# A third fp32 load on the hardware queue at the start, and a planned order with other rules for PSUM banks, scores and values

## The chip, the core and the metric

The kernel runs on one core of a Trainium2 chip. A core has five engines that run side by side, each with its own instruction stream: TensorE (PE in the profile, its weight loads PEld) multiplies matrices and writes to PSUM, VectorE (DVE) and ScalarE (ACT) work on elements and read PSUM, GpSimd (POOL) and SyncE (SP) here mostly issue DMA transfers. PSUM has 8 banks per partition; a bank holds one 128x512 fp32 result. Engines wait for each other by semaphores.

The metric is the time of one execution on the device in microseconds (us), the median of several runs. Before the change it is 298.91 us, with runs from 298.06 to 298.91.

## What is computed

Sliding-window causal attention over 8 batches, 8 heads, 576 positions and a head size of 64, followed by a feed-forward block with silu on the 4608 tokens:

```python
scores = scale * np.matmul(q, k.transpose(0, 1, 3, 2))
rel = pos[:, None] - pos[None, :]
scores = np.where((rel >= 0) & (rel < 64), scores, -1e9)
attn = softmax(scores)                       # per row
x = np.matmul(attn, v)  ->  tokens x 512     # heads side by side
h = x @ w_in                                 # 512 -> 2048
out = (h * sigmoid(h)) @ w_out               # 2048 -> 512, fp32
```

Inputs are fp32 in DRAM; the kernel multiplies in bf16.

## The kernel before, in words

**Attention.** The window is 64 wide, so a block of 64 queries needs two blocks of keys. A unit is three query blocks of a batch. For batches 1 to 7 a unit takes all eight heads: 48 small matmuls of scores into four banks (`scores`, L331), four exps on ACT (`expo`, L337), four masks on DVE (L340), two times 24 matmuls of values (`values`, L349) into two banks, then reciprocal, product and a transposition on DVE (L356, L359, L363) that leave the result, turned, in the SBUF tile `bridge`. Batch 0 takes one half of the heads at a time and adds its mask as a matmul of a bias (L311) ahead of the scores (L319).

**How q and k of batch 0 arrive.** Two heads of q or k are one tensor of 128 rows; there are four such tensors of q and four of k. Those of heads 0 and 1 are loaded by SP's hardware queue as fp32 rows into `nat` tiles (`load_first`, L232) and cast to bf16 on ACT or DVE (`cast_first`, L235). The other six are loaded by POOL's software queue, which casts on the way (`load_first_cast`, L229). Two tensors at a time are turned by PE (`turn_first`, L282) and copied out of PSUM (`lift`, L289). Later batches come through POOL (`load_rows`, L239) and are turned by DVE (L246). POOL also loads v (L253), w_in (L259) and w_out (L265). It issues a load only once the eighth load before it has landed.

**Feed-forward block.** Tokens are taken in nine tiles of 512. For a tile the first layer makes 16 groups of four matmuls (`first_layer`, L369), each group into one bank; ACT empties the bank with a silu into a tile `g` (`silu`, L375). The second layer then makes four groups of 16 matmuls (`second_layer`, L381); ACT or DVE copies each bank out (L387) and SP stores it (L391). The first two tiles are cut into narrower groups. The first layers of the nine tiles appear in the profile as nine stretches of first-layer matmuls.

**What sets the order.** The kernel holds a small planner, the class `Plan`. Every piece of work is added with a class, an assumed time on each engine that may do it, the pieces it depends on, and for PE work a pool of PSUM banks. `Plan.run` steps through assumed time: whenever an engine is free, it takes the piece of the best rank whose dependencies are seen, whose gate lets it pass, and for which its pool has enough idle banks. The instructions are then issued in that order. On the chip the order is fixed; only semaphores decide when each instruction starts. Assumed times thus act on the order and on the choice of banks, not on the waits themselves.

Banks 0 to 3 are named `at`, 4 to 7 `mp`. Scores of later batches take `at`; values take the pool `pv`, which is banks mp0 and mp1; the feed-forward block takes the pool `mp`, all four of mp0 to mp3, and prefers mp2 and mp3. Of the idle ones it takes the one idle the longest. In the kernel before, once no values are left to plan, every piece may take any of the eight banks. From tile 2 the silus and copies count as seen 0.22 us after their assumed end; before, 0.08 us.

Two gates place scores and values between the matmuls of the feed-forward block. `scores_may_run` lets a unit's scores run when enough second-layer matmuls are left in the tile (`more`: 14, or 3 for the first unit of batch 3 and later). `values_wait` holds scores back while values are ready; `values_may_run` holds values from batch 2 on back until the scores may follow them, or until few second-layer matmuls are left. Between the units PE is filled up with feed-forward matmuls of the tile before.

In the first 17 us PE runs matmuls on a blank tile whenever nothing else is ready (`warm`, L612).

## Time and profile before

| | |
|---|---|
| median of 3 runs | 298.91 us (298.06 to 298.91) |
| profiled execution, its own time | 298.06 us |
| its span in the profile | 296.3 us |
| granted TensorE clock, mean | 0.999 |
| PE busy, 3609 matmuls | 285.1 us |
| ACT busy | 176.2 us |
| DVE busy | 138.6 us |
| POOL busy | 117.8 us |
| first-layer matmuls into mp banks (L369) | 109.8 us |
| second-layer matmuls into mp banks (L381) | 99.4 us |
| POOL's software queue | 18.07 MB, 65.9% of 16 engines' span |
| SP's hardware queue | 10.03 MB, 9.5% |

A line of the timeline gives the start in us from the span's start, the duration, the engine, the line of the kernel, the operation, the tile written and the tiles read, shapes and the number of instructions merged into it; in brackets stands how long the engine was idle before it and who ended that. The end of a matmul is modelled (a 128x512 one shows 0.38 us, while the next starts 0.216 us after it), so a busy PE row can overlap the next. Idle time of less than 0.15 us is not listed. In the chain of waits each row is a start, a duration and what ran; "issue" is time in which nothing that the profile shows was waited for. In the list of waits the numbers are total us, how many, and the longest.

### The profile page before, as it was taken

The numbers are of one execution on the slowest core, as the hardware profiler recorded it, in microseconds if no ns is written. First come the engines' busy times: TensorE is split into PE (matmuls) and PEld (weight loads), VectorE is DVE, ScalarE is ACT, GpSimd is POOL, SyncE is SP. The second block draws the span as 40 slices with busy tenths as digits, with TensorE's granted clock in tenths as the row PEclk, the third lists the DMA queues.
The fourth block names the chain that finished last, engine by engine and source line by source line (L and its number), as shares of the span: only waits on it lengthen the run. The fifth ranks groups of instructions, "written<-read, shape, count | busy, mean of one in ns | idle before, by whom it ended". The sixth has DMA issues, their size and how long they took to land.

```text
span 296.3 us, 8502 instructions
## 1 busy us (share of the span) xinstructions
PE 285.1 (96%) x3609; PEld 150.2 (51%) x3641; DVE 138.6 (47%) x340; ACT 176.2 (59%) x340; POOL 117.8 (40%) x175
## 2 busy tenths in 40 slices
PE   8989999899999999999999999999999999999996
PEld 4566644775444544445444454455445444444444
DVE  3682488987885379367922791075205300000000
ACT  5788655787367746764578438753767176217512
POOL 8977896979898968970500000000000000000000
PEclk9999999999999999999999999999999999999999
DMA  8999999999999999993910110011101100010012
GB/s 168 170 201 172 151 160 171 233 138 136 175 176 131 116 177 156 143 117 85 124 28 3 40 71 35 2 38 73 38 0 38 73 35 3 35 71 35 2 71 72
DMA packets 82982, 28.64 MB, mean 97 GB/s; under 512 B 72448, under 2 KB 78208, under 8 KB 82944
## 3 DMA queue, kind: packets, MB, share of 16 engines
q0 software_dynamic: 77184, 18.07, 65.9%
q1 hardware_dynamic: 5760, 10.03, 9.5%
q8 instruction: 28, 0.46, 0.7%
q14 instruction: 10, 0.08, 0.1%
HBM read 36.70 MB, written 9.44 MB: 156 GB/s over the span
## 4 chain that ended last, share of the span: by engine, by line
PE 81%; DMA 7%; POOL 7%; issue 3%; ACT 1%; POOLq 0%; ACTq 0%
PE mp L369 30%; PE mp L381 29%; PE at L381 8%; PE at L369 6%; PE mp L349 3%; PE at L331 3%; DMA w_in_sb<-in_moe_w_in_dram 3%; DMA w_out_sb<-in_moe_w_out_dram 2%; DMA vv<-in_v_dram 2%; POOL nat L239 2%; POOL vv L253 2%; POOL w_out_sb L265 1%; POOL natb L229 1%; POOL w_in_sb L259 1%; ACT ot L387 0%
## 5 line engine op out<-in xcount | busy, mean ns | idle before, releaser
L369 PE MATMUL mp<-bridge,w_in_sb 128*128 128x512 bf16 (+5 forms) x612 | 109.8, 337 | 2.3 <-ACT g L375 0.8
L381 PE MATMUL mp<-w_out_sb,g 128*128 128x512 bf16 (+2 forms) x450 | 99.4, 370 | 4.3 <-issue 3.3
L369 PEld LDWEIGHTS <-w_in_sb 128*128 128x128 bf16 x696 | 66.6, 98 | 61.0 <-issue 2.4
L375 ACT ACTIVATE g<-mp 128x512 bf16<-128x512 f32 (+5 forms) x153 | 77.2, 514 | 24.8 <-PE mp L369 23.6
L381 PEld LDWEIGHTS <-g 128*128 128x128 bf16 x608 | 56.3, 98 | 62.5 <-issue 1.3
L337 ACT ACTIVATE e<-at 128x384 bf16<-128x384 f32 x90 | 38.0, 495 | 24.8 <-PE at L331 24.3
L239 POOL DMA_DIRECT2D nat<-in_k_dram x56 | 34.6, 631 | 13.2 <-DMA vv<-in_v_dram 6.9
L340 DVE TENSOR_TENSOR e<-e,mask 128x384 bf16<-128x384 bf16 x84 | 25.3, 346 | 24.6 <-ACT e L337 24.4
L253 POOL DMA_DIRECT2D vv<-in_v_dram x32 | 31.9, 1016 | 9.7 <-PE mp L349 8.4
L239 POOL DMA_DIRECT2D nat<-in_q_dram x56 | 35.1, 649 | 1.6 <-DMA w_in_sb<-in_moe_w_in_dram 1.3
L387 ACT COPY ot<-mp 128x512 f32<-128x512 f32 (+2 forms) x28 | 15.8, 568 | 33.3 <-issue 16.2
L356 DVE RECIPROCAL rc<-mp 128x6 f32<-128x6 f32 x43 | 7.8, 189 | 39.3 <-PE mp L349 38.7
L381 PE MATMUL at<-w_out_sb,g 128*128 128x512 bf16 (+1 forms) x126 | 25.6, 359 | 0.1
L363 DVE STREAM_TRANSPOSE bridge<-ox 128x384 bf16<-128x384 bf16 x48 | 24.8, 553 | 0.0
L246 DVE STREAM_TRANSPOSE kt<-nat 128x576 bf16<-128x576 bf16 x28 | 20.7, 783 | 6.3 <-DMA nat<-in_k_dram 6.3
L246 DVE STREAM_TRANSPOSE qt<-nat 128x576 bf16<-128x576 bf16 x28 | 20.9, 787 | 3.5 <-DMA nat<-in_q_dram 3.4
L359 DVE TENSOR_TENSOR ox<-mp,rc 128x384 bf16<-128x384 f32 x43 | 21.5, 539 | 0.1
L369 PE MATMUL at<-bridge,w_in_sb 128*128 128x512 bf16 x84 | 19.3, 379 | 0.0
L387 ACT COPY ot<-at 128x512 f32<-128x512 f32 (+1 forms) x8 | 4.4, 546 | 20.7 <-PE at L381 20.7
L349 PEld LDWEIGHTS <-e 128*32 128x32 bf16 x1152 | 11.1, 95 | 9.3 <-issue 5.5
L375 ACT ACTIVATE g<-at 128x512 bf16<-128x512 f32 x21 | 12.3, 597 | 4.8 <-PE at L369 4.8
L349 PE MATMUL mp<-vv,e 128*32 128x65 bf16 x1032 | 12.9, 194 | 0.3 <-ACT e L337 0.2
(57 smaller groups left out, 122.7 us busy)
## 6 DMA issues: line engine op xcount, KB each, us to landing
out_dram<-ot SPq DMA_DIRECT2D x35, 256.0 KB, 2.0
vv<-in_v_dram POOLq DMA_DIRECT2D x32, 144.0 KB, 5.6
nat<-in_q_dram POOLq DMA_DIRECT2D x56, 72.0 KB, 4.5
nat<-in_k_dram POOLq DMA_DIRECT2D x56, 72.0 KB, 4.1
w_out_sb<-in_moe_w_out_dram POOLq DMA_DIRECT2D x8, 256.0 KB, 6.2
w_in_sb<-in_moe_w_in_dram POOLq DMA_DIRECT2D x6, 256.0 KB, 7.3
w_in_sb<-in_moe_w_in_dram POOLq DMA_DIRECT2D x4, 128.0 KB, 5.9
natb<-in_q_dram POOLq DMA_DIRECT2D x3, 144.0 KB, 4.8
```

Source lines behind the costliest of these rows:

```text
L239: nc.gpsimd.dma_start(out=nats[i][32 * h:32 * h + 32].rearrange("p (m x) -> p m x", m=NB), in_=(q, k)[kk][b, 4 * a + h].rearrange("(m p r) ...
L246: nc.vector.transpose(out=to[:, (2 * a + part) * S:(2 * a + part + 1) * S].rearrange("x (m t r) -> x m r t", t=32, r=2), in_=nats[i].rearr ...
L253: queue[e].dma_start(out=vv[b % NV][:, 2 * g0 + 1:2 * g1 + 1:2, 0:D], in_=v[b].rearrange("h s d -> (h s) d").rearrange("(g p) d -> p g d", ...
L337: nc.scalar.activation(out=es[n % NE], in_=at_six(bank), func=ACTF.Exp, scale=scale)
L340: nc.vector.tensor_mul(es[n % NE], es[n % NE], mask0 if g == 0 else mask)
L349: nc.tensor.matmul(at_pv(bank)[32 * h:32 * h + 32, x, t], lhsT=e_of(b, a, n, h)[:, x, 32 * t:32 * t + 32], rhs=vv[b % NV][:, (4 * a + h) * ...
L359: nc.vector.tensor_mul(oxs[n % NOX], at_pv(bank)[:, :, :, 0:D], rcs[n % NRC].unsqueeze(3).to_broadcast([128, 3, 2, D]))
L363: nc.vector.transpose(out=bridge[:, n0:n0 + 3, 2 * a:2 * a + 2].rearrange("x t s (u i) -> x t s u i", u=2), in_=oxs[n % NOX].rearrange("p ...
L369: nc.tensor.matmul(banks[bank["bank"][0]][:, 0:hi - lo], lhsT=w_in_sb[:, c, ft * 128:(ft + 1) * 128], rhs=bridge[:, (j * TT + lo) // 64:(j ...
L375: nc.scalar.activation(out=gts[gt][:, lo:hi], in_=banks[bank["bank"][0]][:, 0:hi - lo], func=ACTF.Silu)
L381: nc.tensor.matmul(banks[bank["bank"][0]][:, 0:hi - lo], lhsT=gts[gt][:, m * 128:(m + 1) * 128], rhs=w_out_sb[:, f, lo:hi], start=(f == 0) ...
L387: copies[e](out=ots[ot][:, lo:hi], in_=banks[bank["bank"][0]][:, 0:hi - lo])
```

## The change

Six things change:

1. `load_first` takes the pair of heads as an argument, and the first three entries of `FIRST_LOADS` (q of heads 0 and 1, k of heads 0 and 1, q of heads 2 and 3) go through SP's queue and are cast on ACT or DVE. The class "early" covers the four that follow.
2. In the planner, an SP load of the start is never slowed by POOL's transfers, counts as seen 0.5 us after its transfer instead of 1.2, and the assumed transfer is 0.69 us for all three.
3. Work takes banks from its own pool to the end; the switch to all eight banks goes.
4. Silus and copies count as seen 0.08 us after their assumed end in all tiles.
5. Scores run while more than 14 second-layer matmuls are left, for every unit; `values_wait` goes.
6. Values have no gate.

The order is planned anew with this, so instructions move on all engines.

```diff
-                            idle = [i for i in self.pools[op["pool"] if head["pv"] < len(self.queues["pv"]) else "all"] if i not in kept and self.done(self.banks[i])]
+                            idle = [i for i in self.pools[op["pool"]] if i not in kept and self.done(self.banks[i])]
...
-                        busy = pipe[True] > begin
+                        busy = pipe[True] > begin and c != "ld0"
...
-                        op["seen"] = pipe[False] + {"ld0": 1.2, "st": 1.2}.get(c, 3.0)
+                        op["seen"] = pipe[False] + {"ld0": 0.5, "st": 1.2}.get(c, 3.0)
...
-    def load_first(i, kk):
-        nc.sync.dma_start(out=nats[i][:, 0:2 * S].bitcast(FP32), in_=two(0, kk))
+    def load_first(i, u, kk):
+        nc.sync.dma_start(out=nats[i][:, 0:2 * S].bitcast(FP32), in_=two(u, kk))
...
-    def scores_may_run(whole, more):
+    def scores_may_run(whole):
...
-        return rest > (more if whole else 6)
+        return rest > (14 if whole else 6)
...
-    def next_of(ops):
...
-    def values_wait(b):
-        pv = next_of(p.queues["pv"])
-        return b > 2 and pv is not None and p.done(pv["deps"])
-
-    def values_may_run():
-        s, op = next_of(p.queues["s"]), next_of(op for op, _, _ in moe[scores_may_run.i:])
-        if s is None or op is None or not p.done(op["deps"]):
-            return True
-        kind, rest = next((kind, rest) for o, kind, rest in moe[scores_may_run.i:] if o is op)
-        return kind == 2 and rest < 5 or p.done(s["deps"]) and scores_may_run(True, s["more"])
...
-            if u == 0:
+            if (what, u) in FIRST_LOADS[0:3]:
...
-                ld = p.add("ld0", {"SP": 0.45}, lambda _, i=i, kk=kk: load_first(i, kk), dma=-0.15 if kk == 0 else 0.7)
+                ld = p.add("ld0", {"SP": 0.45}, lambda _, i=i, u=u, kk=kk: load_first(i, u, kk), dma=0.69)
...
-                ca = p.add("early" if (what, u) in FIRST_LOADS[2:6] else "dma0", {"POOL": 0.6}, lambda _, w=w, u=u, kk=kk: load_first_cast(w, u, kk), dma=0.74)
+                ca = p.add("early" if (what, u) in FIRST_LOADS[3:7] else "dma0", {"POOL": 0.6}, lambda _, w=w, u=u, kk=kk: load_first_cast(w, u, kk), dma=0.74)
...
-        more = 3 if b > 2 and g == 0 else 14
...
-                  lat=0.1, gate=lambda: scores_may_run(whole, more) and not values_wait(b), pool="at" if b else "all", b=b, nb=2 * na)
-        s["more"] = more
+                  lat=0.1, gate=lambda: scores_may_run(whole), pool="at" if b else "all", b=b, nb=2 * na)
...
-                   gate=values_may_run if b > 1 else None,
...
-                            silu(bank, g, lo, hi), [op] + free_gt.get(g, []), lat=0.22 if j > 1 else 0.08, table="silu"))
+                            silu(bank, g, lo, hi), [op] + free_gt.get(g, []), table="silu"))
...
-                           [op, free_ot.get(ot)], lat=0.22 if j > 1 else 0.08)
+                           [op, free_ot.get(ot)])
```

## The prediction, on record before the result

> **What bounds the kernel now.** I read the page first: shares by engine, then the costliest groups.
>
> ```profile
> PE 285.1 (96%) x3609; PEld 150.2 (51%) x3641; DVE 138.6 (47%) x340; ACT 176.2 (59%) x340; POOL 117.8 (40%) x175
> ...
> L375 ACT ACTIVATE g<-mp 128x512 bf16<-128x512 f32 (+5 forms) x153 | 77.2, 514 | 24.8 <-PE mp L369 23.6
> ```
>
> TensorE (PE) fills the span, and the silu evictions of L375 wait for it. So a change is worth what it adds to or takes from PE's waits. Next, PE's waits from 83 us to the end:
>
> ```profile
> PE mp L381 <- issue: 2.4, 15, 0.2
> PE mp L369 <- issue: 0.2, 1, 0.2
> ```
>
> No line names another engine. In these 213 us there is nothing left to gain, and every new wait is paid in full. Before 83 us there are such waits; the timeline of the start shows them:
>
> ```profile
> 9.86 0.47 PE L282 MATMUL at<-ident,natb 128*64 128x128 bf16 x9 [0.28 <-DMA natb<-in_k_dram]
> ...
> 17.59 1.73 PE L369 MATMUL mp<-bridge,w_in_sb 128*128 128x192 bf16 x16 [0.41 <-DVE bridge L363]
> 19.97 1.25 PE L369 MATMUL mp<-bridge,w_in_sb 128*128 128x192 bf16 x13 [0.65 <-DMA w_in_sb<-in_moe_w_in_dram]
> ...
> 42.14 1.02 PE L381 MATMUL mp<-w_out_sb,g 128*128 128x512 bf16 x4 [0.28 <-DMA w_out_sb<-in_moe_w_out_dram]
> ...
> 47.20 0.59 PE L381 MATMUL mp<-w_out_sb,g 128*128 128x512 bf16 x2 [0.27 <-DMA w_out_sb<-in_moe_w_out_dram]
> ```
>
> At 19.97, 42.14 and 47.20 PE waits for weights that POOL's queue brings. The landings set these moments, not PE. From the starts of neighbouring matmuls the last two waits cost 0.44 and 0.43 us (0.655 and 0.650 us from one start to the next, less the 0.216 pitch).
>
> **Part 1: banks of the first layer, stretches three to nine.** Pools fall back to four banks at the end, and an eviction counts as seen 0.08 us after its end instead of 0.22. I compared the two kernels' orders of instructions. For 512-wide groups of four first-layer matmuls, the old order never returns to a bank earlier than three groups later. The new one goes mp3, mp2, mp1, mp0, mp3, mp2, mp1, mp3, mp2 and then only to and fro between two banks. This gives 7 returns after two groups in each of six stretches; in the ninth 15, of which 14 follow a first-layer use of the bank. Does a bank come free in two groups? The third stretch and its evictions:
>
> ```profile
> 83.38 13.98 PE L369 MATMUL mp<-bridge,w_in_sb 128*128 128x512 bf16 x64 [0.16 <-issue]
> ...
> 87.96 0.60 ACT L375 ACTIVATE g<-mp 128x512 bf16<-128x512 f32 x1 [0.28 <-PE mp L369]
> 88.82 0.60 ACT L375 ACTIVATE g<-mp 128x512 bf16<-128x512 f32 x1 [0.27 <-PE mp L369]
> ```
>
> Matmul pitch is (13.98 - 0.38) / 63 = 0.216 us, a group 0.863. The sixth group starts at 83.38 + 5 x 0.863 = 87.70 and its silu at 88.82, 1.12 later. The silu takes 0.60. What silu's end to the next matmul in the bank costs is seen on the chain, where narrow groups already alternate on two banks:
>
> ```profile
> 54.09 0.34 ACT g L375
> 54.43 0.04 issue
> 54.47 0.82 PE mp L369 x8
> ```
>
> It is 0.04 to 0.05 (0.050 in the records). The loop is 1.123 + 0.597 + 0.050 = 1.770 us, two groups take 1.727: **0.044 us missing**. A late first matmul moves its neighbour too, so only each second return pays: 4 of 7, 24 in six stretches. In the ninth the first three silus wait for PE alone. Such silus start 0.06 sooner, as the jump from 268.33 to 269.26 (0.93 for 0.863) shows:
>
> ```profile
> 268.33 0.60 ACT L375 ACTIVATE g<-mp 128x512 bf16<-128x512 f32 x1 [0.27 <-PE mp L369]
> 269.26 0.60 ACT L375 ACTIVATE g<-at 128x512 bf16<-128x512 f32 x1 [0.33 <-PE at L369]
> ```
>
> Their loop closes in 1.71, without a wait, and 6 returns pay. Together 30 x 0.044 = **+1.3 us**. Behind the waiting matmul stands all of PE, but weight loads go ahead; ACT has 0.27 us idle per group, so silus do not fall further behind. The price lies between 0 (the loop has room; PE has no wait here to lose, so no gain) and 30 x 0.10 = 3.1 (one more step of 0.06 in each loop). I take 0.044, since the silu rows have this very shape. In the second layer two banks cost nothing: a group of 16 lasts 3.45 us, its copy 0.59. The table load ahead of each stretch stays hidden, because the first four groups use four banks in stretches three to eight, and the ninth has no table load.
>
> The Trainium skill, page "Perfetto Trace Analysis", section "Matmul Optimizations", says to use all 8 PSUM banks. It speaks against this edit but gives no price; applied without the row it would also charge the second layer, where the row shows none.
>
> **Part 2: order of scores and values from batch 2.** Before, 15 times values and the next scores run back to back, 3 times each stands alone. After: 12, 6 and 6. From the last wide matmul's start to the next one's, less its pitch, records show 1.289 us for the pair, 0.808 for values alone, 0.576 for scores alone. Splitting costs 0.808 + 0.576 - 1.289 = 0.095, three times 0.29. Five of the old pairs show 0.02 more each (values waiting for the mask), 0.1 in all, which the new order avoids: batch 2 has it already, with values 18 matmuls after the scores and no wait. Net **+0.2 us**. If the masks were late everywhere, 0.4 us (the longest such wait of the weight loads) in 18 units would be an upper bound of 7; batches 2 and 7 show zero, so I leave that to the tail of the range.
>
> **Part 3: q of heads 2 and 3 through SP's queue.** POOL loses one issue (0.68 us), SP gains one ahead of its first store (50 us later, free), ACT gains a cast (0.67; queued behind it are the first copies to qt and kt, which wait longer for PE). Each POOL load waits for the landing of the eighth before it; one load fewer at the head shifts both alike, and the issues stay where the landings put them. The two changed delays of SP's loads act on the planned order alone. What the DMA engines do, in slices of 0.3 us from 0 to 12 us:
>
> ```profile
> GB/s 0 0 0 0 0 38 92 84 330 407 384 419 319 192 188 142 96 188 200 200 192 188 184 169 192 173 169 176 173 163 160 146 155 157 153 154 157 155 203 148
> ```
>
> First only SP's two loads run, at about 400 GB/s written as fp32; then POOL's casting loads at about 190 as bf16, which is 380 read. The third tensor costs 295 KB / 400 = 0.74 us there, against 147 KB / 190 = 0.78 here. No row shows both queues in full flow, so bounds: if it rides free, all of POOL's loads land 0.78 earlier and the two w_out waits give back 0.78 of their 0.87; if they share, 0. I take 0, because the engines move both at nearly the same rate of fp32 read and SP's third load would start when POOL's first are due. Had POOL's queue been pushed back by the same 0.74, it would cost 0.74, but the load it no longer carries cancels that.
>
> The Trainium skill, page "DMA: Bandwidth & Descriptors", section "Issuing engines are not separate DMA queues", says that loads of different issuers share the 16 engines and interleave, and only issue time is saved. By it this part's gain would also be nothing; no row here shows the two queues together.
>
> The order at the start costs something. All three earlier transpositions now come first, behind 18 warm-ups instead of 15 (0.99 + 18 x 0.32 = 6.75 us, later than the cast, 4.35 + 0.74 + 0.67 = 5.8). The first scores then follow the fourth transposition, which waits for the last k (9.86 row): from 10.5 instead of 8.6 us. So all 12 exps come after 11.3: seven at 0.40 to 14.1, the copy that waits for v until 14.68, then five at 0.41 from 15.26, ending at 17.3 instead of 16.5. The first silu comes at 18.8 instead of 17.95, the fifth group's third matmul at 19.97: just when the weights land. The last bridges end at about 21.4 instead of 21.3. Bounds: 0 (absorbed here and by the w_out waits) to +0.8 (nothing absorbed). I take **0**.
>
> **Sum.** 1.3 + 0.2 + 0 = +1.5 us on the profiled execution's own 298.06 (span 296.3 and 1.8 around it): 299.6. It was the lowest of three runs, 0.85 below the median; on the median of 298.91 the forecast is **300.4 us**.
>
> **Rivals.**
> - *The loop closes.* If matmuls see a bank's release 0.044 us sooner than in the narrow loops, or the silus start at once as those three of the last stretch do, part 1 vanishes: +0.2, **299.1**, no measurable change. For it: the margin is 2.5% of the loop. Against: 0.050 recurs wherever ACT held PE up. This is the case on the other side; it decides when the loop is under 1.727 us.
> - *The third load rides free.* For it: the queues differ in the packets they make. Against: both rates above. -0.78 + 1.5 = +0.7: **299.6**. With the first rival too, -0.6: **298.3**.
> - *The late start is not absorbed.* +0.8 more: **301.2**. For it: the bridges have 0.15 us of room at 21.46. Against: two w_out waits of 0.87 follow.
>
> **How the numbers follow.** About 0.3% (0.9 us) is what a measurement of this kernel can tell from no change. Chances: forecast 0.55 (own range 299.8 to 301.1), loop closes 0.15, rides free 0.14, both 0.08, late start 0.08. Forecast and late start are slower, with a little lost at the edge: 0.60. The loop closing, the free ride and half of both are within 0.9: 0.29. The rest, with what I do not see, is faster: 0.11. The range runs from both rivals together (298.3, less 0.2) to the late start and some (301.2 + 0.5).
>
> **What would show it.** In the profile after: PE's waits in stretches three to nine with gaps before the first-layer matmuls put down to L375, or, since 0.044 is too short for a listed gap, stretches of 64 matmuls 0.18 us longer than 13.98 and the ninth 0.27; silus on the to-and-fro banks 0.907 apart at every second one; w_out waits at the same times within 0.3 us; first silu near 18.8. Wrong it would be if the stretches keep 13.98, if w_out lands 0.7 us earlier, or if values wait for masks.

## The result and the profile after

The changed kernel takes **302.14 us** (median of six runs, 300.13 to 303.33) against 298.31 us for the kernel before in the same comparison (six runs, 297.36 to 298.91): a ratio of **1.0118**, 95% interval 1.0079 to 1.0157. It is slower, as forecast, but by 3.8 us where 1.5 were forecast, and the time lies above the stated range, which ended at 301.7.

The profiled execution took 302.37 us. Its span is 300.6 us, 4.3 more than before. First the rows of the page after that answer to those of the page before:

```profile
span 300.6 us, 8485 instructions
PE 287.4 (96%) x3609; PEld 150.4 (50%) x3641; DVE 139.4 (46%) x340; ACT 176.8 (59%) x341; POOL 117.0 (39%) x174
...
L375 ACT ACTIVATE g<-mp 128x512 bf16<-128x512 f32 (+5 forms) x174 | 89.5, 523 | 30.9 <-PE mp L369 29.6
...
nat<-in_q_dram SPq DMA_DIRECT2D x2, 288.0 KB, 4.7
```

The records show the same 3609 matmuls on PE and one cast more on ACT. The row of silus alone cannot be set beside the one before: it has gathered other groups (174 instead of 153), because the old order spread its banks over two names.

To find where 4.3 us went, I cut the span in three: **start** (up to the first matmul of the third stretch of first-layer matmuls), **loop** (from there to the end of the last copy out of PSUM, L387), and **end** (the rest of the span). The start is read from the timeline, the other two from the chain and the span.

| | start | loop | end | sum |
|---|---|---|---|---|
| before | 83.38 | 210.38 | 2.54 | 296.3 |
| after | 85.21 | 212.01 | 3.38 | 300.6 |
| difference | +1.83 | +1.63 | +0.84 | +4.3 |

**The loop** does what the prediction says. The chain of waits after, rows of first-layer matmuls between the third stretch and the ninth (start, duration, what ran):

```profile
85.21 14.14 PE mp L369 x64
116.50 14.00 PE mp L369 x64
147.66 13.99 PE mp L369 x64
178.82 13.99 PE mp L369 x64
...
268.90 14.08 PE mp L369 x64
```

The same rows before, as far as the chain has them as one piece:

```profile
83.38 13.98 PE mp L369 x64
115.00 13.81 PE mp L369 x64
145.88 13.81 PE mp L369 x64
```

The first of each list holds 0.16 us of idle time ahead of it. The others grew from 13.81 by 0.18 to 0.19, and the ninth by 0.27: four and six gaps of 0.044 us. In the records PE stands still for 41 to 46 ns at exactly these 30 places, 1.33 us in all. The list of PE's waits from 83 us on names no other engine, before or after; 0.044 us is too short to be listed there.

**The start** went otherwise. The timelines of ACT and PE after, from 3 us on:

```profile
3.68 1.35 ACT L235 CAST natb<-nat 128x576 bf16<-128x576 f32 x2 [1.66 <-DMA nat<-in_q_dram]
...
8.12 0.67 ACT L235 CAST natb<-nat 128x576 bf16<-128x576 f32 x1 [3.09 <-DMA nat<-in_q_dram]
```

```profile
8.85 1.05 PE L282 MATMUL at<-ident,natb 128*64 128x128 bf16 x17 [2.33 <-ACT natb L235]
9.58 2.23 PE L282 MATMUL mp<-ident,natb 128*64 128x128 bf16 x36
12.49 0.69 PE L282 MATMUL at<-ident,natb 128*64 128x128 bf16 x18
19.65 1.04 PE L369 MATMUL mp<-bridge,w_in_sb 128*128 128x192 bf16 x8
...
44.40 1.02 PE L381 MATMUL mp<-w_out_sb,g 128*128 128x512 bf16 x4 [0.23 <-DMA w_out_sb<-in_moe_w_out_dram]
```

The cast of the third tensor starts at 8.12, since that tensor landed only at 8.10 us (5.1 was assumed). PE waits 2.33 us for it. Then PE is slow as well: 36 transposing matmuls last 2.23 us at 9.58. The table by stretches shows why; its columns are the stretch, its length, the busy time of PE, PEld, DVE, ACT and POOL with the number of instructions, the granted clock of PE, the DMA share and GB/s:

```profile
5.00:10.00 5.00, 2.67 (x32) 1.76 (x31) 1.99 (x6) 1.20 (x3) 5.00 (x6) 0.90 1.31 184
10.00:15.00 5.00, 5.00 (x85) 3.06 (x83) 3.77 (x7) 3.58 (x7) 4.19 (x7) 0.76 2.04 174
```

The same stretches before:

```profile
5.00:10.00 5.00, 4.72 (x83) 2.80 (x82) 3.81 (x8) 2.87 (x6) 4.93 (x7) 1.00 1.48 176
10.00:15.00 5.00, 4.95 (x161) 2.85 (x158) 3.12 (x9) 4.13 (x10) 4.33 (x8) 1.00 1.97 175
```

The granted clock is 0.76 from 10 to 15 us, where it was 1.00 before. (In the records of the clock this and the 0.90 are one piece: half the clock for 3.41 us, from 9.02 to 12.43.) The first matmul of the first layer comes at 19.65 instead of 16.84, 2.8 us later. Of that 1.0 is absorbed further on: the wait of 0.65 us for w_in is gone, of the two waits for w_out one is left, with 0.23 us listed, and the start ends 1.83 us late.

**The end** is longer by 0.84 us although the last store does the same work. SP's last instructions look at eight semaphores of its transfers in a fixed row, and the records show which of them the last store is on. It is the last of the row before, so all others have been looked at by then: landed at 295.37, seen at 295.38, end of the span 296.29. After, SP issues 41 transfers instead of 40, the last store falls on the first semaphore of the row, and the other looks follow its landing: landed at 298.83, first look 298.85, last look 299.70, end 300.6.

### The profile page after: what moved, and what is told of

Same layout as the page of the kernel before. It is cut to its first block, busy times and chain, and to the rows that moved or that the text cites. A ratio compares the mean times of both kernels' runs of the same rounds, so it can differ in the third digit from the quotient of the medians.

```text
span 300.6 us, 8485 instructions
## 1 busy us (share of the span) xinstructions
PE 287.4 (96%) x3609; PEld 150.4 (50%) x3641; DVE 139.4 (46%) x340; ACT 176.8 (59%) x341; POOL 117.0 (39%) x174
## 4 chain that ended last, share of the span: by engine, by line
PE 82%; DMA 8%; POOL 6%; issue 3%; ACT 1%; POOLq 0%; ACTq 0%
PE mp L381 39%; PE mp L369 37%; DMA w_out_sb<-in_moe_w_out_dram 5%; PE at L331 3%; PE mp L349 3%; DMA w_in_sb<-in_moe_w_in_dram 2%; POOL vv L253 2%; POOL w_in_sb L259 1%; POOL nat L239 1%; POOL w_out_sb L265 1%; POOL natb L229 1%; ACT ot L387 0%; ACT g L375 0%; PE at L349 0%; POOL ident L188 0%
## 5 line engine op out<-in xcount | busy, mean ns | idle before, releaser
L369 PE MATMUL mp<-bridge,w_in_sb 128*128 128x512 bf16 (+5 forms) x696 | 128.6, 342 | 1.8 <-ACT g L375 1.2
L381 PE MATMUL mp<-w_out_sb,g 128*128 128x512 bf16 (+2 forms) x576 | 124.2, 368 | 4.1 <-issue 3.3
L375 ACT ACTIVATE g<-mp 128x512 bf16<-128x512 f32 (+5 forms) x174 | 89.5, 523 | 30.9 <-PE mp L369 29.6
L387 ACT COPY ot<-mp 128x512 f32<-128x512 f32 (+2 forms) x36 | 20.2, 563 | 62.1 <-PE mp L381 42.8
L340 DVE TENSOR_TENSOR e<-e,mask 128x384 bf16<-128x384 bf16 x84 | 26.0, 348 | 50.2 <-ACT e L337 49.7
L337 ACT ACTIVATE e<-at 128x384 bf16<-128x384 f32 x89 | 36.9, 497 | 16.0 <-PE at L331 15.9
L299 DVE COPY vv<-vv 64x576 bf16<-64x576 bf16 (+1 forms) x14 | 7.3, 524 | 11.7 <-DMA nat<-in_k_dram 9.2
L349 PE MATMUL mp<-vv,e 128*32 128x65 bf16 x1032 | 12.2, 194 | 0.0
L331 PE MATMUL at<-qt,kt 32*128 32x64 bf16 x1008 | 11.6, 190 | 0.0
L331 PEld LDWEIGHTS <-kt 32*128 32x128 bf16 x1008 | 9.3, 92 | 4.3 <-issue 3.8
```

The lines of the kernel that those rows point to most:

```text
L331: nc.tensor.matmul(at_six(op["bank"][h])[:, a, x], lhsT=kt[b % NK][r, at:at + 128], rhs=qt[b % NK][r, at:at + 64], start=(s == a == x == 0 ...
L337: nc.scalar.activation(out=es[n % NE], in_=at_six(bank), func=ACTF.Exp, scale=scale)
L340: nc.vector.tensor_mul(es[n % NE], es[n % NE], mask0 if g == 0 else mask)
L349: nc.tensor.matmul(at_pv(bank)[32 * h:32 * h + 32, x, t], lhsT=e_of(b, a, n, h)[:, x, 32 * t:32 * t + 32], rhs=vv[b % NV][:, (4 * a + h) * ...
L369: nc.tensor.matmul(banks[bank["bank"][0]][:, 0:hi - lo], lhsT=w_in_sb[:, c, ft * 128:(ft + 1) * 128], rhs=bridge[:, (j * TT + lo) // 64:(j ...
L375: nc.scalar.activation(out=gts[gt][:, lo:hi], in_=banks[bank["bank"][0]][:, 0:hi - lo], func=ACTF.Silu)
```

## The experiments

Theory after the result: three separate costs. (1) Two banks in the loop cost 30 x 0.044 us, and the new order of scores and values 0.2 to 0.3. (2) The third load lands late beside POOL's transfers, and the start pays for that. (3) The number of SP's transfers sets where the last store stands among the looks at the end. Rivals are named with each run. The table has all runs: the three parts of the profiled execution, the median, and the ratio to runs of the kernel before on the same chip, with its 95% interval. SP's queue gets three loads at the start where "loads" is 3.

| run | banks | loads | start | loop | end | median | ratio |
|---|---|---|---|---|---|---|---|
| before | old | 2 | 83.38 | 210.38 | 2.54 | 298.31 | 1 |
| after | new | 3 | 85.21 | 212.01 | 3.38 | 302.14 | 1.0118 (1.0079 to 1.0157) |
| two loads | new | 2 | 82.94 | 212.55 | 2.54 | 301.01 | 1.0118 (1.0094 to 1.0142) |
| banks back | old | 3 | 84.39 | 210.66 | 3.39 | 300.48 | 1.0095 (1.0075 to 1.0115) |
| one more transfer | old | 2 | 83.78 | 210.39 | 3.42 | 299.30 | 1.0053 (1.0037 to 1.0069) |
| new gates alone | old | 2 | 83.29 | 210.66 | 2.54 | 298.40 | 1.0017 (1.0002 to 1.0033) |
| third load alone | old | 3 | 84.97 | 210.41 | 3.40 | 300.32 | 1.0062 (1.0040 to 1.0085) |
| POOL waits | new | 3 | 87.81 | 213.20 | 3.38 | 306.16 (one run) | |
| planner told | new | 3 | 86.08 | 212.71 | 3.40 | 303.03 | 1.0158 (1.0130 to 1.0185) |
| 0.22 everywhere | old | 2 | 83.25 | 210.41 | 2.53 | 298.11 | 0.9997 (0.9981 to 1.0013) |
| seven more transfers | new | 3 | 85.12 | 212.00 | 2.50 | 301.08 | 1.0101 (1.0069 to 1.0133) |
| banks alone | new | 2 | 83.41 | 211.94 | 2.53 | 299.65 | 1.0066 (1.0042 to 1.0090) |
| w_out earlier | old | 2 | 86.04 | 210.41 | 2.53 | 301.17 | 1.0103 (1.0066 to 1.0140) |
| other third tensor | old | 3 | 85.31 | 210.39 | 2.49 | 300.51 | 1.0110 (1.0063 to 1.0157) |
| unread third load | old | 3 | 84.36 | 210.39 | 2.57 | 300.00 | 1.0055 (1.0037 to 1.0072) |
| other third, planned soon | old | 3 | 85.29 | 210.39 | 2.49 | 299.62 | 1.0041 (1.0023 to 1.0059) |

The parts are from one execution each. Those of the loop and the end repeat to some hundredths among kernels of the same banks, the same gates and the same place of the last store; the three loops above 212.5 hold something more, which their sections tell. The start differs by some tenths even between kernels with the same loads.

### The change without its third load

```diff
-            if (what, u) in FIRST_LOADS[0:3]:
+            if (what, u) in FIRST_LOADS[0:2]:
...
-                ca = p.add("early" if (what, u) in FIRST_LOADS[3:7] else "dma0", ...
+                ca = p.add("early" if (what, u) in FIRST_LOADS[2:6] else "dma0", ...
```

> The changed kernel with the third load back on POOL's queue; the planner's new rules for banks, scores and values stay. Theory (the third load is what delays the start, and one more SP transfer is what lengthens the end): the first transposition starts at 5.7 us again instead of 8.85, the first first-layer matmul near 17, the clock stays at 1.00 from 5 to 15 us, the third stretch of first-layer matmuls starts within 0.4 us of 83.4 (85.2 after the change), the time from the last copy's end to the end of the span is 2.5 us again instead of 3.4. The 30 bank waits of 0.044 us stay. Time about 1.5 us above before, ratio near 1.005. Rival (the new order of transpositions and first scores makes the start late, not the load): the third stretch still starts near 85, ratio near 1.010.

In the profile the start falls from 85.21 to 82.94 and the end from 3.38 to 2.54, as expected: both go with the third load. (With two loads the planned order of PE at the start is nearly that of before again, so this run alone doesn't tell the load from the order; the unread load below does.) The median followed only in part: 3.2 us above before, where the change is 3.8 above, and the ratios are equal. The profiled execution, 299.8, is the lowest of the four. In it the loop is 0.54 longer than after. Two evictions start late, a silu (L375) and a copy (L387), and PE pays for both. The chain of waits of this run through the first of them:

```profile
176.54 6.94 PE mp L369 x32
183.47 0.02 issue
183.49 0.02 ACTq L375
183.51 0.32 issue
183.84 0.61 ACT g L375
184.44 0.04 issue
184.48 6.33 PE mp L369 x28
```

ACT waits 0.32 us at 183.51 for nothing that the profile shows, and the chain goes through its silu. The other on ACT's timeline, with the copy of the same kind before it:

```profile
263.52 0.59 ACT L387 COPY ot<-mp 128x512 f32<-128x512 f32 x1 [2.87 <-PE mp L381]
267.25 0.59 ACT L387 COPY ot<-mp 128x512 f32<-128x512 f32 x1 [3.15 <-PE mp L381]
```

More on this under the banks alone.

### The change with the old banks

The three lines of the pools and of 0.08 are put back; all the rest is the changed kernel.

```diff
-                            idle = [i for i in self.pools[op["pool"]] if i not in kept and self.done(self.banks[i])]
+                            idle = [i for i in self.pools[op["pool"] if head["pv"] < len(self.queues["pv"]) else "all"] if i not in kept and self.done(self.banks[i])]
...
-                            silu(bank, g, lo, hi), [op] + free_gt.get(g, []), table="silu"))
+                            silu(bank, g, lo, hi), [op] + free_gt.get(g, []), lat=0.22 if j > 1 else 0.08, table="silu"))
```

> The changed kernel with the old rules for banks alone (evictions of tile 2 and later seen after 0.22 us, all eight banks open at the end). Theory: no return to a bank after two groups of 512 in stretches three to nine, each stretch 13.81 us from first start to last as before, 30 x 0.044 = 1.3 us less than the changed kernel, so about 2.5 us above before (ratio 1.008); start and end as late as in the changed kernel. Rival (the to-and-fro costs more than its visible gaps, for instance through the clock): 2 us or more less than the changed kernel.

The loop falls from 212.01 to 210.66. The chain of waits shows the stretches at the length of before, two of five such rows:

```profile
115.50 13.81 PE mp L369 x64
146.48 13.81 PE mp L369 x64
```

The 0.28 that are left over 210.38 are the new order of scores and values.

The start is 84.39 and not as late as in the changed kernel, against the expectation. The order of PE's matmuls up to the first layer is the same in both. But here PE waits 1.75 us for the third tensor, where it waited 2.33 after the change, and the clock stays at 1.00 from 5 to 15 us. The wait on PE's timeline:

```profile
8.67 0.69 PE L282 MATMUL at<-ident,natb 128*64 128x128 bf16 x17 [1.75 <-ACT natb L235]
```

So of the 1.83 us at the start some 1.0 come at full clock, and the other 0.8 go with the longer wait and the halved clock of that execution. (The run with seven more transfers has this order too; its clock fell, and its start is 85.12.)

### The kernel before with one more transfer of SP

A load of 2 KB that nothing reads; SP then has 41 transfers, as after. (It is planned after the first exps, but nothing on the chip holds it: SP issues it at 1.64 us.)

```diff
+    tiny = keep.tile([128, 4], FP32, name="tiny")
+    p.add("tiny", {"SP": 0.45}, lambda _: nc.sync.dma_start(out=tiny, in_=v[0, 0, 0:128, 0:4]), exps[0], dma=0.0)
```

> The kernel before, with one tiny load more on SP's queue (128 x 4 fp32 into a tile that nothing reads), issued long before the first store. Theory (the last store's semaphore is now the first of those that SP checks at the end, so the other checks come after its landing): from the last copy's end to the end of the span 3.4 us instead of 2.5, everything before it the same, time +0.8 us, ratio 1.003. Rival (the longer end comes from the last stores being slower behind two banks): no difference, ratio 1.000.

The end goes from 2.54 to 3.42. Two kilobytes that nobody waits for cost 0.88 us there. With the 0.40 by which this profile's start is later, it is 1.3. The ratio, 1.0053, is above the 1.003 expected; what the start has of that is not explained.

### The kernel before with the new gates alone

```diff
-        more = 3 if b > 2 and g == 0 else 14
+        more = 14
...
-                  lat=0.1, gate=lambda: scores_may_run(whole, more) and not values_wait(b), ...
+                  lat=0.1, gate=lambda: scores_may_run(whole, more), ...
...
-                   gate=values_may_run if b > 1 else None,
+                   gate=None,
```

> The kernel before, with the new gates for scores and values alone: 6 single scores, 6 single values and 12 pairs from batch 2 on instead of 3, 3 and 15. Theory: 3 x 0.095 = 0.29 us more for the splits, up to 0.1 less waiting for masks: +0.2 us, ratio 1.001, not to be told from none. Rival (values wait for masks in the new order): over 1 us more, with gaps ahead of the values.

The loop is 210.66, +0.28, what the three more splits were to cost; the 0.1 for waits that go is not to be seen. The values are not late anywhere: the 0.2 of the prediction is right within 0.1.

### The kernel before with the third load alone

```diff
-            if u == 0:
+            if (what, u) in FIRST_LOADS[0:3]:
...
-                ld = p.add("ld0", {"SP": 0.45}, lambda _, i=i, kk=kk: load_first(i, kk), dma=-0.15 if kk == 0 else 0.7)
+                ld = p.add("ld0", {"SP": 0.45}, lambda _, i=i, u=u, kk=kk: load_first(i, u, kk), dma=-0.15 if (kk, u) == (0, 0) else 0.7)
```

> The kernel before with the third load on SP's queue alone; old rules for banks, scores and values. Theory (both queues share the DMA engines and the SP load, which comes last, gets the smaller part): the third load lands near 8 us, not at 5.1; the first transposition of q starts near 8.7; the third stretch of first-layer matmuls starts 0.5 to 2 us later than in the kernel before; the end is 0.84 us longer; nothing between them changes. Time +1.3 to +2.8 us, ratio 1.005 to 1.009. Rival (the load is harmless, what hurt was the new order with the other rules): +0.84 us from the end alone, ratio 1.003.

The load alone, with banks and gates of before, makes the start 1.59 later and the end 0.86 longer. The third tensor lands at 7.94. Here the granted clock is 1.00 all through the start, so the clock is not needed for a late start.

### The change with POOL's first loads held back

POOL copies four columns of the third tensor to a tile that nothing reads, and its loads of q and k wait for that copy. So the third load has none of them beside it. (Three loads of v are issued ahead of the copy; their first packet starts at 4.43 us, near the third load's end.)

```diff
+                if u == 1:
+                    held = [p.add("hold", {"POOL": 0.2}, lambda _, i=i: nc.gpsimd.tensor_copy(out=hold, in_=nats[i][:, 0:4]), [ld])]
...
-                ca = p.add("early" ..., lambda _, w=w, u=u, kk=kk: load_first_cast(w, u, kk), dma=0.74)
+                ca = p.add("early" ..., lambda _, w=w, u=u, kk=kk: load_first_cast(w, u, kk), held, dma=0.74)
```

> The changed kernel in which POOL first copies four columns of the third load's tile into a tile that nothing reads, so that all its own loads are issued after the third load has landed. Theory (sharing): with the engines to itself the third load lands 0.75 us after the second, at about 5.1 us, against 8.1 in the changed kernel; all POOL loads come some 4 us later, so the whole is slower. Rival (a third load in SP's queue is slow by itself): it lands near 8 us here too.

The third cast on ACT, and SP's two loads of q (number, size, median time to landing), in this run:

```profile
5.33 0.67 ACT L236 CAST natb<-nat 128x576 bf16<-128x576 f32 x1 [0.97 <-DMA nat<-in_q_dram]
```

```profile
nat<-in_q_dram SPq DMA_DIRECT2D x2, 288.0 KB, 3.3
```

Nearly by itself the third load lands at 5.31, close to the 5.1 that the prediction assumed; beside POOL's queue at 8.10. The assumed rate was right and the sharing was not. The kernel as such is slower, since POOL's own loads of q and k then land over 4 us later than in the changed kernel.

### The planner told when the third load lands

In the change the planner takes 0.69 us for this transfer. If it knows that the load is late, it can put other work first.

```diff
-                ld = p.add("ld0", ..., dma=0.69)
+                ld = p.add("ld0", ..., dma=0.69 if u == 0 else 3.9)
```

> The changed kernel with the planner told that the third load lands late (3.9 instead of 0.69 us of transfer); loads and all other rules the same. Theory: the load still lands near 8 us; 30 warm-ups instead of 18 fill the wait, so TensorE has no long gap before 9 us and its granted clock stays at 1.00 from 5 to 15 us instead of 0.90 and 0.76; the four transpositions are through by 11.5 instead of 13.1; the third stretch starts 0.3 to 1.3 us earlier than in the changed kernel, limited by the landing of w_out. Rival (the clock and the gap are harmless, since w_out is waited for anyway): the third stretch starts as in the changed kernel, within 0.3 us.

My theory fell here: the start became later, 86.08. The transpositions no longer leave a long gap, but PE waits later, for an exp, as the list of its waits shows, and then the clock drops (columns as above):

```profile
PE at L349 <- ACT e L337: 2.4, 1, 2.4
```

```profile
20.00:25.00 5.00, 4.65 (x54) 4.10 (x55) 4.18 (x11) 3.45 (x10) 2.38 (x4) 0.66 1.40 196
```

This order doesn't repair the start: the wait moved from 6.5 us to 15.6 us, and was as long. The loop is longer as well, because 48 matmuls of values stand behind the first two of the third stretch, 0.58 us that are counted in the start of the changed kernel. (The run with POOL's loads held has 0.58 us of them there, too.)

### The kernel before with 0.22 in all tiles

```diff
-                            silu(bank, g, lo, hi), [op] + free_gt.get(g, []), lat=0.22 if j > 1 else 0.08, table="silu"))
+                            silu(bank, g, lo, hi), [op] + free_gt.get(g, []), lat=0.22, table="silu"))
```

> The kernel before with evictions counted as seen after 0.22 us in all tiles, the first two as well: a try to go below both kernels. Theory: the narrow groups of the second stretch still alternate on two banks (9 returns after two groups instead of 8), so nothing moves by more than 0.3 us, ratio 1.000. Rival (other banks in the first two stretches save the four waits of 0.25 us at 54 to 58 us): up to 1 us less, ratio 0.997.

No difference: 0.9997. The first two tiles have nothing to gain from the old rule.

### The change with seven more transfers of SP

Seven loads of 2 KB that nothing reads: 48 transfers, so the last store is again on the semaphore that is looked at last. (These too are planned after the first exps, but issued from 2.12 to 7.09 us.)

```diff
+    tiny = keep.tile([128, 28], FP32, name="tiny")
+    for i in range(7):
+        p.add("tiny", {"SP": 0.45}, lambda _, i=i: nc.sync.dma_start(out=tiny[:, 4 * i:4 * i + 4], in_=v[0, 0, 0:128, 0:4]), exps[0], dma=0.0)
```

> The changed kernel, and seven further loads of 2 KB each on SP's queue, of data that nothing reads, once the first exp has run. With 48 transfers of SP in place of 41 the last store falls again on the semaphore that SP looks at last, as with 40. Theory (what the third load costs at the end is where the last store stands in the row of the eight last checks): the stretch from the end of the last copy to the end of the span falls from 3.38 us to 2.54 +- 0.05, the start and the loop stay (start of the third stretch of first-layer matmuls at 85.2 +- 0.5, from there to the last copy 212.0 +- 0.5), so 0.84 us less than the changed kernel: ratio to the kernel before 1.0085 +- 0.003. Rival (each further transfer of SP costs at the end): 3.4 us or more, ratio 1.012 or above.

The end falls to 2.50 with more transfers, as the position says and against the rival. Start and loop stay at 85.12 and 212.00. The end of the chain of waits after, and then of this run:

```profile
core 0 of [0], span 300.6 us
...
296.96 0.27 ACT ot L387
```

```profile
core 0 of [0], span 299.6 us
...
296.85 0.27 ACT ot L387
```

From the last copy's end to the span's end it is 3.4 us in the first and 2.5 in the second. The medians alone (ratios 1.0118 and 1.0101, with wide intervals) would not have told them apart.

### The new banks alone

The kernel before, with the three lines of the banks changed as in the change, and nothing else.

> The kernel before with the new bank rules alone: an eviction counts as seen 0.08 us after its end everywhere, and there is no switch to all eight banks at the end. Loads and gates are the old ones. Theory (two banks cost 0.044 us at 30 places, and the end and the start are untouched): the start 83.4 +- 0.3, the loop from 210.4 to 211.7 +- 0.25, the last stretch 2.54; median +1.3 us, ratio 1.0045 (1.003 to 1.006). Rival (in a loop on two banks TensorE also pays for every silu that starts late, as in the run with two loads, where 0.32 and 0.30 were paid beside the 0.044): loop +1.8 us or more, ratio 1.007 to 1.010. The old banks would hide such a silu, since a bank then comes back after three groups at the earliest.

The chain of waits has the stretches of the changed kernel:

```profile
115.19 13.99 PE mp L369 x64
146.86 13.99 PE mp L369 x64
...
267.03 14.08 PE mp L369 x64
```

The loop is 211.94, +1.56: the records show the 30 gaps (1.33), and the planned order shifts with the banks, so that two more pairs of values and scores are split (0.23 left, and two splits were to cost 0.19). The loop is in the theory's range. The median, +1.7, doesn't decide: its ratio of 1.0066 lies between what the theory and the rival gave, and its interval reaches into both.

The rival has a true core, though. Late evictions happen with the old banks too. The run with the third load alone has a late silu; ACT's timeline shows it, and the chain of waits at the same place goes through PE without a break:

```profile
251.02 0.60 ACT L375 ACTIVATE g<-at 128x512 bf16<-128x512 f32 x1 [0.27 <-PE at L369]
252.16 1.18 ACT L375 ACTIVATE g<-at 128x512 bf16<-128x512 f32 x2 [0.55 <-PE at L369]
```

```profile
239.70 2.59 PE at L369 x12
242.29 1.73 PE mp L369 x8
244.02 3.45 PE at L369 x16
```

That silu is 0.28 late (0.55 of idle time for 0.27), and the stretch keeps 13.60 us from its first matmul to its last, the length of all stretches with old banks. With three groups between two uses of a bank the loop has 3 x 0.863 - 1.77 = 0.82 us of room; with two groups it has none. In the sixteen profiles of this study late silus of this kind stand in three with old banks, one each (the third load alone, and the two runs with another third tensor), and no stretch there is longer for it. With new banks there are a late silu and a late copy in the run with two loads, and the same two in that with POOL's loads held. Each of these four evictions makes one stretch 0.28 us longer than its neighbours of the same kind. So this second cost of two banks is shown as a mechanism.

What makes an eviction late is not shown, but the records show where it happens. Counted in ACT's own stream, waits for semaphores included, each of these seven is the 320th or the 448th instruction, and 0.65 to 0.93 us after its start a packet starts on q14, one of the two queues that carry instructions. (Not every eviction at these places is late: the silu at the 448th in the run with the planner told starts on time.) So the loading of ACT's instructions is the suspect; no run here tested it. In the changed kernel and in that with the banks alone, a wait for a semaphore has these two places, and no eviction is late in their profiles. So late evictions don't account for these two medians as far as the records go. Single times of banks alone reach 3.0 us beyond their lowest and those of two loads 1.8; what the longer executions hold is open.

### w_out earlier

The two waits for w_out in the profile before (0.87 us) are the only thing there to gain. Two of these loads go ahead of values of batch 1.

```diff
-    FIRST, SPLIT, SECOND_LOADS = 8, 14, "0w12ww3vwvwvwvww"
+    FIRST, SPLIT, SECOND_LOADS = 8, 14, "0w12ww3vwwvwwvvw"
```

> The kernel before with two of the first weights of the second layer moved ahead of values of batch 1 in POOL's queue, so that TensorE's two waits for w_out (0.87 us together in the profile of before) might go. If they go and no values come late: start of the third stretch 82.5 +- 0.3, ratio 0.997. If the transfers that were moved back are as much needed (the start is bound by the sum of what POOL's queue brings): the same 83.4 +- 0.3 or later, ratio 0.999 to 1.004, with TensorE waiting for v or its transposition instead.

A miss: the start is 2.66 later. One wait for w_out stays (0.84 us at 43.15), and the planned order of batch 1 changed, so that PE waits 2.3 us between 52 and 57 us for banks that ACT and DVE had not emptied.

### Another tensor as the third load

q of heads 6 and 7, which is read last, comes through SP's queue in place of q of heads 2 and 3. Seven loads of 2 KB, read by nothing, keep the end as before.

```diff
-            if u == 0:
+            if u == 0 or (what, u) == ("q", 3):
...
-                ld = p.add("ld0", ..., lambda _, i=i, kk=kk: load_first(i, kk), dma=-0.15 if kk == 0 else 0.7)
+                ld = p.add("ld0", ..., lambda _, i=i, u=u, kk=kk: load_first(i, u, kk), dma=3.5 if u else -0.15 if kk == 0 else 0.7)
```

> The kernel before with another third tensor on SP's queue: q of heads 6 and 7, the last that is needed, in place of q of heads 2 and 3; and seven further loads of 2 KB on SP's queue, of data that nothing reads, so that the last store stands where it stood. Theory (the third load harmed the start because it lands at about 8 us and q of heads 2 and 3 is needed by then): with a tensor that is needed after 10 us POOL's queue is one load shorter and nothing early waits for SP's, so the start of the third stretch is at 83.4 or up to 0.7 us earlier, the last stretch 2.54, ratio 0.997 to 1.001. Rival (any third load of SP slows POOL's first loads, and the start pays for that whatever tensor it is): 84 or later, ratio 1.002 to 1.006.

The start is 85.31, by the rival; the ratio, 1.0110, is above what either gave. But the run was not clean: the 3.5 moved the last transpositions behind three groups of scores and more warm-ups, to 12.86 us (9.86 before). So two more runs were made. (The expectation of the last one speaks of five groups; it is three.)

### A third load that nothing reads

All loads and the planned order of PE are those of the kernel before; beside them SP loads 295 KB (q of heads 4 and 5 once more) into a tile that nothing reads.

```diff
+                if kk == 1:
+                    p.add("ld0", {"SP": 0.45}, lambda _: nc.sync.dma_start(out=unread, in_=two(2, 0)), dma=0.0)
```

> The kernel before, all its loads and its planned order of TensorE kept, and beside them a third load of 295 KB on SP's queue into a tile that nothing reads (q of heads 4 and 5 once more); seven loads of 2 KB on SP's queue as in the run with seven further loads, so that the last store stands where it stood. No instruction waits for the third load: what it costs is what it takes from the other transfers. Theory (a load of SP beside POOL's pushes POOL's first loads back, and the start pays for that): POOL's first load lands at 6.6 +- 0.4 in place of 5.0 and its sixth at 11.2 +- 0.4 in place of 9.8; start of the third stretch 84.4 to 85.0, last stretch 2.5, ratio 1.003 to 1.006. Rival (the start is paid by what waits for the third tensor alone): start 83.4 +- 0.4, ratio 1.000 +- 0.0015.

The timeline of PE before, the first transpositions:

```profile
5.68 0.47 PE L282 MATMUL mp<-ident,natb 128*64 128x128 bf16 x10
...
6.57 0.69 PE L282 MATMUL at<-ident,natb 128*64 128x128 bf16 x18
```

And with the unread load:

```profile
7.23 0.47 PE L282 MATMUL mp<-ident,natb 128*64 128x128 bf16 x9 [1.02 <-DMA natb<-in_q_dram]
...
8.12 0.73 PE L282 MATMUL at<-ident,natb 128*64 128x128 bf16 x18
```

PE waits 1.02 us for POOL's load of q of heads 2 and 3, at a place where it did not wait before. POOL's six loads landed at 7.19, 8.12, 8.90, 9.64, 10.37 and 11.14 instead of 5.00, 6.20, 7.23, 7.96, 9.06 and 9.82. Such landings scatter: in the seven kernels with two loads the first is at 5.00 to 6.32 and the sixth at 9.34 to 10.39, and where it was 10.39 (new gates alone) the start was at 83.29. This run's first and sixth lie beyond these. The start is 84.36, 0.98 later, with the clock at 1.00 all through it, and the ratio 1.0055 (1.6 us) lies within what the theory gave. The rival, that only what reads the third tensor pays, falls. The seven small loads are not what costs: they are issued from 2.11 us on beside POOL's loads, but the changed kernel has its start at 85.12 with them and at 85.21 without.

### Another third tensor, in the planned order of before

As two runs above, with 0.7 for 3.5, so that PE's planned order of the start is that of before.

> The run with q of heads 6 and 7 as third load once more, with the planner told that it lands early, so that TensorE's planned order at the start is that of the kernel before (last transposition before the first scores' second pair, not after five groups of them). Theory (the late start of that run, first silu group at 19.8, came from its own planned order): first matmul of the first layer at 17.0 to 17.6, start of the third stretch 83.4 to 84.0, ratio 1.000 to 1.003. Rival (POOL's first loads pushed back are enough): first matmul at 18 or later, start of the third stretch at 84.5 or later, ratio 1.004 or above.

It misses the theory (start 85.29, first matmul of the first layer at 19.83) and agrees with the rival: POOL's first load lands at 7.15 and PE waits 1.72 us for it, before anything needs the third tensor. The list of PE's waits begins so:

```profile
PE mp L282 <- DMA natb<-in_q_dram: 1.7, 1, 1.7
PE mp L349 <- issue: 1.3, 1, 1.3
```

But a lower clock shares in this late start. The stretches of this run, columns as above:

```profile
5.00:10.00 5.00, 3.28 (x41) 1.79 (x39) 3.49 (x7) 1.99 (x4) 5.00 (x6) 0.79 1.31 183
10.00:15.00 5.00, 5.00 (x95) 3.07 (x95) 2.98 (x6) 3.73 (x9) 3.78 (x6) 0.87 2.14 161
```

With the 3.5 the clock was 1.00 there. So the two starts can't be set side by side, and part of the other run's ratio of 1.0110 may be its planned order. In the median this one is the mildest of the kernels with three loads (1.0041). Its five executions at a clock of 1.0 have a mean of 299.0 us, 0.8 above the mean of before.

## Why the prediction was wrong

- **Part 1 (banks), +1.3 us: right.** Measured 30 gaps of 0.041 to 0.046, 1.33 us, in the stretches and numbers given. "The loop closes" didn't happen.
- **Part 2 (order of scores and values), +0.2 us: right.** 0.28 with the gates alone.
- **Part 3 (the third load), 0 us: this term failed**, and with it the sum. It rested on "the engines move both at nearly the same rate of fp32 read and SP's third load would start when POOL's first are due", and on the landing at about 5.1 that the 6.75 us for the first transposition stood on. The rate holds when the load is nearly alone (5.31). Beside POOL's queue the tensor landed at 8.10, where POOL had brought it at 5.00 before, and the first transposition went on at 8.85. POOL's own loads pay as well: with the unread load its first landed at 7.19, where no kernel with two loads is above 6.32, PE waited 1.02 us for it, and the start came 0.98 later. The forecast set the cost to POOL's queue against the load that it no longer carries. That nearly fits its last load of q or k, at 10.43 for 9.82 before and for 10.39 with the new gates alone, which had no late start; PE's waits are for the early landings. "Rides free" had the wrong sign.
- **"I take 0 (absorbed)" for the order at the start failed with it.** The exps were to run from 11.3 us to 17.3; they ran from 13.94 to 19.30. The last bridge came at 23.41 for 21.4, the first silu at 20.73 for 18.8. The waits for weights did absorb 1.0 us, w_in's as well as w_out's, but 2.8 came in. The rival "the late start is not absorbed" has the right sign at this place, and at +0.8 less than half the size: it kept the early landing. And the clock, which the prediction left at 1.00, was halved for 3.41 us; about 0.8 of the 1.83 us goes with that and the longer wait.
- **"SP gains one ahead of its first store (50 us later, free)" failed.** It counted the issue and not the end of the program: +0.84 us. The profile of before could not show this price, but the records did show that the last store sat on the semaphore that is looked at last, and one more transfer must move it.
- **The rule on shared DMA engines** (the Trainium skill, page "DMA: Bandwidth & Descriptors", section "Issuing engines are not separate DMA queues": transfers of all issuers run on the same 16 engines and interleave) agrees with 8.10 beside POOL and 5.31 nearly alone. The prediction drew from it that nothing is gained; the runs show that interleaving also delays both, and the early work pays.
- **The rule on PSUM banks** (the Trainium skill, page "Perfetto Trace Analysis", section "Matmul Optimizations": use all 8) agrees with the loop: 13.81 us per stretch with three groups between two uses, 13.99 with two.

The parts of the profile sum up: 1.33 + 0.30 in the loop, 1.83 at the start, 0.84 at the end, 4.3 us. So the sum came out in the loop and failed at both ends of the span. No kernel here was measurably below the kernel before.

## What to carry to other kernels

When a load is moved to another queue, don't price its bytes alone: ask what else is in flight at that time, which of the two lands first, and what is the first reader of the one that loses. Where one engine sets the time, give each of its buffers one turn more than the loop needs; two turns that miss by 0.044 us cost at every second turn, and pass on every late start of the engine that empties them. And count the transfers of the queue that stores the result: one more can lengthen the end.

## What the runs showed of the hardware that was not expected

- **A short gap can lower the clock for microseconds.** After PE's 2.33 us without work at 6.5 us the records show half the clock for 3.41 us, from 9.02 on. The other three profiles with such a piece have the same 3.41 us, after gaps of 2.42 (the planner told), 2.27 (seven more transfers) and 1.72 us (the other third tensor, planned soon). The length of the gap alone doesn't decide: in the run with the old banks put back, 1.75 us left the clock at 1.00. Of the six executions of the changed kernel three had a mean clock of 0.992 to 0.994 and took 302.2 to 303.3 us; three had 0.999 to 1.0 and took 300.1 to 302.1. Of the executions of the run with the other third tensor planned soon, five had 0.993 or 0.994 (mean 299.8) and five 1.0 (mean 299.0). None of the kernel before in the later comparisons was below 0.998. So a wait at the start is paid a second time, in part of the executions.
- **Two queues in flight delay both.** 295 KB nearly alone took 0.87 us (from k's landing at 4.44 to 5.31 with POOL's loads held back); beside POOL's queue they landed 2.8 us later and pushed that queue's sixth load back by 1.32 us, or 0.75 to 1.80 against all kernels with two loads. The two together also move less: from 4.25 to 6.75 us, with the casting loads counted twice for their fp32 read, the records sum up to 259 to 313 GB/s in the kernels with three loads in flight beside POOL's first of q and k, and to 314 to 362 in those with two.
- **The looks at the end of the program** depend on where the last store stands: 2.5 us from the last copy to the end of the span if it is on the last semaphore, 3.4 if on the first.
- **Evictions on ACT that start 0.28 us late** stood at the 320th or 448th instruction of ACT's stream wherever one was found from 83 us on: silus and copies, some of them with nobody waiting, as a copy in the kernel before at 177.12 us.
